# An attention stage in front of two expert layers: masking from PSUM, full-height V products, fp32r flips, and a new order of all steps

## The chip, the cores and the metric

The kernel runs on one core of a Trainium2 chip. The metric is the device time of one execution in microseconds, the median over runs. The engines are TensorE (PE; its weight loads are listed apart as PEld), VectorE (DVE), ScalarE (ACT), GpSimd (POOL) and SyncE (SP), which issues all DMAs here. Each engine works through its own queue in the order in which the program wrote it.

## The reference

Attention over 4 batches x 8 heads, 576 positions, head size 64, with a threshold instead of a full softmax, and then two pairs of dense layers on the 2304 tokens. Cut to what matters:

```python
scores = (1 / sqrt(64)) * q @ k.T                      # 576 x 576 for each head
thresh = max(scores, axis=-1) - tau
scores = where(scores >= thresh, scores, -1e9)
attn   = exp(scores - max(scores)); attn /= sum(attn) + 1e-9
x      = heads side by side of (attn @ v)              # 2304 x 512
h = x @ w_in;  x = (h * sigmoid(1.702 * h)) @ w_out    # 512 -> 2048 -> 512
h = x @ w2_in; y = max(0.01 * h, h) @ w2_out           # 512 -> 2048 -> 512
```

All is fp32, and the weights come as fp64. Precision is kept by splitting an operand into a high half in fp32r (a 32-bit format that TensorE takes in one product) and a low half, the difference.

## The kernel before, in words

Attention goes by head pairs, 16 of them; a pair has two heads of 576 rows, which make nine row tiles of 128 (t = 0 to 8; tile 4 holds the last 64 rows of both heads). For each pair the program has about 130 named steps, each a few instructions on one engine:

- `Lk`, `Lq`, `Lv` load, `dkh`, `dkl`, `dqh`, ... (`divide`, L372 and L377, POOL) split into halves. `fk0` to `fq2` (`flip`, L384, PE) transpose the split q and k, 18 tiles of 128 x 128, `ek`, `eq` (ACT) copy them out of PSUM, `sw` swaps halves of k by DMA.
- For each tile t: `Q` (`scores`, L430, PE) writes minus the scores into one of two PSUM buffers named `s`; `R` (`row_min`, L458, DVE) finds the minimum of the row and writes a copy of the scores to SBUF (`sc`, three buffers); `E` (`exponent`, L471, ACT) takes the exponential from PSUM, behind which the PSUM buffer is free; `T` (`threshold`, L478, in five groups of one or two tiles, four on POOL and one on DVE) adds tau; `S` (`mask`, L492, DVE) multiplies the exponential by "copy of the score <= threshold" and sums the row.
- `P` (`flip_probs`, L513, PE) transposes the masked tile into one of four PSUM banks named `t`; `w` (L535, ACT) copies it to SBUF, `h` (L544, ACT; L540, POOL, for tile 2) makes the high half, `l` (L551, POOL; L549, DVE, for tiles 4 and 6) the low half. `F`, `x`, `y` do the same with the last 64 columns.
- `V` (`values`, L586 and L593, PE) multiplies by v: for each of two row groups (256 and 320 columns), two heads and two halves, four products over 128 rows and one over the 64 rows that are left. `a`, `b` add the halves; `ia`, `ib`, `rb`, `N`, `c` (L662) multiply by the inverse of the row sums and write x.

The order is written out by hand: the table `START` gives each step a number, for the first and last pairs in tables of their own and for the others in one table that is shifted by `PERIOD` from pair to pair; the steps are sorted by these numbers, and thus each engine's queue is made. The steps of two or three neighbouring pairs are interleaved. Into the tables of pair 0 are also written the first six weight blocks of the first layer: `G` loads one, `A` to `K` build fp32 from fp64 bits (L311 on ACT, L313, L315, L319 and L323 on DVE), `H` and `M` split it (ACT, POOL).

The two layers follow from 396 us on: 512-column products on PE, the activation on ACT and DVE, halves on ACT and POOL. Nothing there is changed.

Of the kernel before, what the change touches and what calls it, by code (L numbers as in the profile page):

```python
# [8 lines left out]
F32 = mybir.dt.float32  # L9
F32R = mybir.dt.float32r  # L10
# [24 lines left out]
LO = ("P", "P", "PP", "P", "D", "P", "D", "P", "P")  # L35


THR_ENGINE = "PDPPP"
VB, PPB, SCB = 1, 3, 3
WARM = 8  # L40
PERIOD = 17190
# [21 lines left out]
    },  # L63
    0: {
        "G00": 584, "LkB": 1059, "LkA": 2359, "LqB": 2834, "LqA": 4134, "khB": 4232, "A00": 4592, "Lt": 4609,
# [24 lines left out]
    },  # L90
# [18 lines left out]
    },  # L109
# [130 lines left out]
def attention_moe_moe(  # L240
# [20 lines left out]

    ident = cp.tile([P, P], F32, name="ident")
    make_identity(nc, ident)
    xx_all = cp.tile([P, NCB, NTOK], F32, name="x")
    x = [xx_all[:, c, :] for c in range(NCB)]


# [721 lines left out]
```

## Time and profile before

| | |
|---|---|
| median of 3 runs | 1204.96 us (1204.79 to 1207.99) |
| the profiled execution | 1204.73 us, span 1203.0 us |
| PE, PEld busy over the span | 97%, 81% |
| DVE, ACT, POOL busy over the span | 57%, 49%, 57% |
| last `c` step of attention | 396.4 us after the span's start |

The shares are averages over two unlike stages: in the first third DVE and POOL are over 90% busy, behind it they are at some 40%, and PE is at 98% to 99%.

### The profile page before, as it was taken

The numbers are of one execution on the slowest core, as the hardware profiler recorded it, in microseconds if no ns is written. First come the engines' busy times: TensorE is split into PE (matmuls) and PEld (weight loads), VectorE is DVE, ScalarE is ACT, GpSimd is POOL, SyncE is SP. The second block draws the span as 40 slices with busy tenths as digits, with TensorE's granted clock in tenths as the row PEclk, the third lists the DMA queues.
The fourth block names the chain that finished last, engine by engine and source line by source line (L and its number), as shares of the span: only waits on it lengthen the run. The fifth ranks groups of instructions, "written<-read, shape, count | busy, mean of one in ns | idle before, by whom it ended". The sixth has DMA issues, their size and how long they took to land.

```text
span 1203.0 us, 17030 instructions
## 1 busy us (share of the span) xinstructions
PE 1165.1 (97%) x6169; PEld 970.7 (81%) x6169; DVE 685.8 (57%) x1376; ACT 588.0 (49%) x1090; POOL 688.5 (57%) x606
## 2 busy tenths in 40 slices
PE   6889999999999899999999999999999999999998
PEld 6677888888877688888888888888888888888886
DVE  7999999999999433433534434442343443444222
ACT  6778888888876444333323323344443333333221
POOL 6899999999987655433333433365543433343221
PEclk8999999999998999999999999999999999999999
DMA  4422322312210111101101111110120111110022
GB/s 133 122 66 60 84 56 69 81 50 76 64 40 18 53 36 53 53 18 53 53 25 47 53 36 37 52 53 25 47 57 31 36 53 36 53 36 1 35 62 62
DMA packets 47620, 62.38 MB, mean 52 GB/s; under 512 B 10544, under 2 KB 39216, under 8 KB 47536
## 3 DMA queue, kind: packets, MB, share of 16 engines
q1 hardware_dynamic: 47536, 61.29, 17.9%
q8 instruction: 49, 0.80, 0.3%
q14 instruction: 35, 0.29, 0.1%
HBM read 47.71 MB, written 4.72 MB: 44 GB/s over the span
## 4 chain that ended last, share of the span: by engine, by line
PE 69%; POOL 18%; DVE 6%; issue 4%; ACT 1%; DMA 1%; SPq 0%; DVEq 0%; POOLq 0%; ACTq 0%
PE h L829 31%; PE y L876 16%; PE y L874 15%; POOL ptg0l L551 4%; POOL ptg1l L551 4%; POOL thr L478 2%; PE pv L586 2%; DVE pp L492 2%; POOL rb L635 1%; POOL khl L377 1%; PE s L430 1%; POOL qhl L372 1%; POOL vhl L377 1%; PE pp L513 1%; PE pv L593 1%
## 5 line engine op out<-in xcount | busy, mean ns | idle before, releaser
L845 POOL TENSOR_TENSOR gl<-gf,gh 128x512 fp32r<-128x512 f32 (+1 forms) x160 | 210.1, 1313 | 471.6 <-ACT gh L844 454.9
L841 DVE TENSOR_TENSOR gf<-h,gf 128x512 f32<-128x512 f32 (+1 forms) x80 | 51.0, 637 | 242.0 <-ACT gf L840 242.0
L838 DVE TENSOR_TENSOR gf<-h,gf 128x512 f32<-128x512 f32 (+1 forms) x80 | 51.0, 637 | 231.7 <-ACT gf L837 231.7
L829 PE MATMUL h<-xl,wih 128*128 128x512 f32 (+1 forms) x640 | 159.9, 369 | 3.0 <-POOL xl L818 3.0
L829 PE MATMUL h<-xh,wih 128*128 128x512 f32 (+1 forms) x640 | 158.8, 369 | 1.7 <-ACT xh L817 1.6
L840 ACT ACTIVATE gf<-h 128x512 f32<-128x512 f32 (+1 forms) x80 | 44.4, 555 | 233.7 <-PE h L829 230.6
L829 PE MATMUL h<-xh,wil 128*128 128x512 f32 (+1 forms) x640 | 157.5, 368 | 0.0
L837 ACT ACTIVATE gf<-h 128x512 f32<-128x512 f32 (+1 forms) x80 | 44.3, 554 | 228.1 <-PE h L829 225.0
L492 DVE SCALAR_TENSOR_TENSOR pp<-sc,thr,e 128x576 f32<-128x576 f32 x128 | 151.3, 1191 | 2.3 <-POOL thr L478 1.8
L829 PEld LDWEIGHTS h<-xl,wih 128*128 128x128 f32 x640 | 113.9, 188 | 26.1 <-POOL xl L818 6.1
L829 PEld LDWEIGHTS h<-xh,wih 128*128 128x128 f32 x640 | 114.6, 188 | 24.5 <-ACT xh L817 3.4
L829 PEld LDWEIGHTS h<-xh,wil 128*128 128x128 f32 x640 | 113.8, 189 | 20.0
L471 ACT ACTIVATE e<-s,m 128x576 f32<-128x576 f32 x144 | 107.1, 744 | 34.4 <-DVE sc L458 18.9
L844 ACT CAST gh<-gf 128x512 fp32r<-128x512 f32 (+1 forms) x160 | 92.7, 579 | 56.6 <-DVE gf L841 32.3
L874 PE MATMUL y<-gh,woh 128*128 128x512 f32 (+1 forms) x320 | 117.0, 370 | 2.1 <-DVE x L894 1.2
L874 PE MATMUL y<-gh,wol 128*128 128x512 f32 (+1 forms) x320 | 116.4, 368 | 0.0
L876 PE MATMUL y<-woh,gh 128*128 128x512 f32 x288 | 112.4, 390 | 0.0
L876 PE MATMUL y<-wol,gh 128*128 128x512 f32 x288 | 112.3, 390 | 0.0
L458 DVE TENSOR_SCALAR_CACHE_REDUCE sc<-s 128x576 f32<-128x576 f32 x144 | 107.1, 750 | 3.9 <-PE s L447 1.6
L430 PE MATMUL s<-kt,qt 128*128 128x288 f32 x512 | 99.2, 319 | 9.6 <-ACT e L471 7.4
L551 POOL TENSOR_TENSOR ptg0l<-raw,ptg0h 128x512 fp32r<-128x512 f32 x64 | 91.5, 1431 | 0.3 <-ACT ptg0h L544 0.3
L874 PE MATMUL y<-gl,woh 128*128 128x512 f32 (+1 forms) x320 | 88.5, 368 | 0.0
(122 smaller groups left out, 2261.9 us busy)
## 6 DMA issues: line engine op xcount, KB each, us to landing
w<-in_moe_w_in_dram SPq DMA_DIRECT2D x32, 512.0 KB, 3.7
w<-in_moe_w_out_dram SPq DMA_DIRECT2D x32, 512.0 KB, 3.5
kt<-kt SPq DMA_DIRECT2D x30, 288.0 KB, 4.1
kn<-in_k_dram SPq DMA_DIRECT2D x16, 256.0 KB, 2.8
qn<-in_q_dram SPq DMA_DIRECT2D x16, 256.0 KB, 2.8
vn<-in_v_dram SPq DMA_DIRECT2D x16, 256.0 KB, 3.0
out_dram<-o SPq DMA_DIRECT2D x20, 128.0 KB, 2.4
out_dram<-o SPq DMA_DIRECT2D x8, 256.0 KB, 2.2
```

The source lines that it names most:

```text
L430: nc.tensor.matmul(sc[:, a, 0:HALF], lhsT=w, rhs=kt[n][:, c : c + HALF], start=n == 0, stop=n == 1)
L458: nc.vector.tensor_scalar(out=split(r["sc", t], 2), in0=r["s", t][:, :, 0:HALF], scalar1=1.0, scalar2=3.0e38, op0=ALU.mult, op1=ALU.min, a ...
L471: nc.scalar.activation(split(e, 2), r.pop(("s", t))[:, :, 0:HALF], AF.Exp, bias=r["m"][:, t : t + 1], scale=-1.0)
L492: nc.vector.scalar_tensor_tensor(out=dst, in0=r.pop(("sc", t)), scalar=r["thr"][:, t : t + 1], in1=r.pop(("e", t)), op0=ALU.is_le, op1=ALU ...
L551: nc.gpsimd.tensor_tensor(out=lo, in0=split(st[p].pop(("raw", t)), 4), in1=hi, op=ALU.subtract)
L829: nc.tensor.matmul(h, lhsT=wt[:, c * P : (c + 1) * P], rhs=xx[c], start=i == 0 and c == 0, stop=i == 2 and c == NCB - 1)
L838: nc.vector.tensor_tensor(out=gf, in0=h, in1=gf, op=ALU.mult)
L841: nc.vector.tensor_tensor(out=gf, in0=h, in1=gf, op=ALU.max)
L844: nc.scalar.copy(gh, gf)
L845: nc.gpsimd.tensor_tensor(out=gl, in0=gf, in1=gh, op=ALU.subtract)
L874: nc.tensor.matmul(ys[e][:, 0:w], lhsT=wt[:, at_e], rhs=g, start=first, stop=last)
L876: nc.tensor.matmul(ys[e], lhsT=g[:, at_e], rhs=wt, start=first, stop=last)
```

## The change

- `R` is a reduction that reads the scores in PSUM and writes only the minimum; there is no copy `sc`. `S` reads the scores in PSUM, so a buffer `s` is free only behind `S`.
- `T` is one step for each tile, all nine on DVE.
- Tile 2's high half is made by ACT from PSUM, as for the other tiles.
- v's buffer is one lasting tile that is zeroed once; the last 64 rows of the second head lie in a tenth tile, so that the fifth product of each `V` step runs over all 128 rows, of which 64 are zero. v's split covers ten tiles.
- `flip` is a matmul in fp32r with an fp32r identity in place of a transpose of fp32 bits. `corner` uses two matmuls over all 128 rows in place of a transpose and a matmul over 64.
- All tables of `START` are new, and so is `PERIOD` (17190 to 21444); the numbers serve as sort keys only. Pair 12 uses the common table now, pair 3 too. The weight blocks begin behind the first thresholds of pair 0 (`G00`) and their steps lie among those of pairs 1 to 9; before, four of the six were converted among the first steps and two at the end of attention.

```diff
-LO = ("P", "P", "PP", "P", "D", "P", "D", "P", "P")
-THR_ENGINE = "PDPPP"
-VB, PPB, SCB = 1, 3, 3
-PERIOD = 17190
+LO = ("P", "P", "P", "P", "D", "P", "D", "P", "P")
+PPB = 3
+PERIOD = 21444
...
+    identr = cp.tile([P, P], F32R, name="identr")
+    nc.vector.tensor_copy(identr, ident)
...
+        vn = at.tile([P, 640], F32, name="vn")
+        nc.gpsimd.memset(vn, 0.0)
...
+            c = 320 if nm == "v" else 0
...
-                    nc.sync.dma_start(t[64 * j : 64 * j + 64, 256:320], src[b, h0 + j, 512:576, :])
+                    nc.sync.dma_start(t[64 * j : 64 * j + 64, 256 + c * j : 320 + c * j], src[b, h0 + j, 512:576, :])
...
-            src = st[p][nm + "n"][:, 0:576].rearrange("p (t d) -> p t d", d=D)
+            n = 10 if nm == "v" else 9
+            src = st[p][nm + "n"][:, 0 : n * D].rearrange("p (t d) -> p t d", d=D)
...
-                nc.tensor.transpose(pt[:, n * P : (n + 1) * P], st[p][nm][:, t, :].bitcast(F32), ident)
+                nc.tensor.matmul(pt[:, n * P : (n + 1) * P], lhsT=st[p][nm][:, t, :], rhs=identr, start=True, stop=True)
...
-            r["sc", t] = at.tile([P, S], F32, tag="sc", name=f"sc{p}_{t}", bufs=SCB)
-            nc.vector.tensor_scalar(
-                out=split(r["sc", t], 2),
-                in0=r["s", t][:, :, 0:HALF],
-                scalar1=1.0,
-                scalar2=3.0e38,
-                op0=ALU.mult,
-                op1=ALU.min,
-                accum_out=small(p, "m")[:, t : t + 1],
+            nc.vector.tensor_reduce(
+                out=small(p, "m")[:, t : t + 1], in_=r["s", t][:, :, 0:HALF], axis=mybir.AxisListType.XY, op=ALU.min
             )
...
-        def threshold(p, n):
-            c = slice(THR[n][0], THR[n][-1] + 1)
-            (nc.vector if THR_ENGINE[n] == "D" else nc.gpsimd).tensor_scalar(
+        def threshold(p, t):
+            c = slice(t, t + 1)
+            nc.vector.tensor_scalar(
...
             nc.vector.scalar_tensor_tensor(
-                out=dst,
-                in0=r.pop(("sc", t)),
+                out=split(dst, 2),
+                in0=r.pop(("s", t))[:, :, 0:HALF],
                 scalar=r["thr"][:, t : t + 1],
-                in1=r.pop(("e", t)),
+                in1=split(r.pop(("e", t)), 2),
...
-            nc.tensor.transpose(pt[0:64, 256:320], src[0:64, :], ident[0:64, 0:64])
-            nc.tensor.matmul(pt[64:128, 256:320], lhsT=src[64:128, :], rhs=ident[64:128, 64:128], start=True, stop=True)
+            for h in range(2):
+                d = slice(64 * h, 64 * h + 64)
+                nc.tensor.matmul(pt[d, 256:320], lhsT=src, rhs=ident[:, d], start=True, stop=True)
...
-            for j in range(4):
+            for j in range(5):
                 nc.tensor.matmul(
                     pv,
                     lhsT=r["v"][:, 5 * h + j, :],
-                    rhs=r["pt", gi][n][:, j, h, :],
-                    start=n == 0 and j == 0,
-                    stop=False,
+                    rhs=r["pt", gi][n][:, j, h, :] if j < 4 else r["rt", gi][n],
+                    start=first and j == 0,
+                    stop=not first and j == 4,
                 )
-            nc.tensor.matmul(
-                pv, lhsT=r["v"][rows, 4, :], rhs=r["rt", gi][n][rows, :], start=False, stop=n == 1
-            )
```

The order of the common table in the part that the prediction walks through, by queue (a prime marks the pair before, `+` the pair behind):

```
PE:  Q0 P5' N0' fk0+ P6' Q8' fk2+ Q1 fk1+ P0 P7' fq0+ Q2 F1' P8' Q3 P1 V100' V101' Q4 P2 Q5 ...
DVE: R0 S7' T0 c0' S0 R8' T8' R1 S8' l6' T1 S1 R2 ia1' y1' T2 R3 S2 ib1' T3 S3 b10' R4 ...
ACT: E7' w5' E0 h5' h6' ek0+ ek2+ E8' ek1+ h0 E1 w0 w7' h7' x1' eq0+ E2 h8' E3 ...
```

## Rows read from the trace of the kernel before

**Rows 1.** Windows: length, busy us (count) by engine, clock, DMA share, GB/s.
```profile
10.00:60.00 50.00, 39.23 (x237) 32.77 (x236) 48.81 (x98) 36.17 (x68) 39.99 (x34) 0.90 0.41 116
...
200.00:250.00 50.00, 49.69 (x339) 41.80 (x338) 48.74 (x115) 43.57 (x82) 50.00 (x47) 1.00 0.24 60
...
360.00:396.90 36.90, 33.95 (x185) 25.47 (x183) 30.87 (x71) 24.32 (x47) 26.04 (x26) 0.91 0.09 30
...
600.00:1203.00 603.00, 595.20 (x2805) 498.43 (x2804) 226.55 (x388) 192.85 (x350) 231.89 (x182) 1.00 0.14 42
```
**Rows 2.** The chain that ended last: start us, us, what.
```profile
117.72 1.64 POOL rb L635 x3
...
228.37 1.64 POOL rb L635 x3
```
**Rows 3.** Waits, four pairs, 150.2 to 238.7 us: total, times, longest.
```profile
PEld s L430 <- ACT e L471: 1.4, 4, 0.3
PEld pp L513 <- DVE xs L612: 0.8, 4, 0.2
```
**Rows 4.** VectorE by line and form, same stretch: busy us, mean ns | idle before.
```profile
L492 DVE SCALAR_TENSOR_TENSOR pp<-sc,thr,e 128x576 f32<-128x576 f32 x33 | 38.2, 1166 | 0.1
L458 DVE TENSOR_SCALAR_CACHE_REDUCE sc<-s 128x576 f32<-128x576 f32 x36 | 26.8, 751 | 1.2 <-PE s L447 0.7
...
L492 DVE SCALAR_TENSOR_TENSOR pm<-sc,thr,e 128x576 f32<-128x576 f32 x4 | 5.6, 1405 | 0.0
L549 DVE TENSOR_TENSOR ptg1l<-pp,ptg1h 128x512 fp32r<-128x512 f32 x8 | 5.5, 685 | 0.1
...
L478 DVE TENSOR_SCALAR thr<-m,tau_p 128x2 f32<-128x2 f32 x4 | 0.9, 214 | 0.0
```
**Rows 5.** The mask's line, whole run: duration ns min/median/max, first and last start.
```profile
L492 DVE SCALAR_TENSOR_TENSOR pp<-sc,thr,e x128: 798/1197/1892, 14.1 to 381.6; 128x576 f32<-128x576 f32 x128
```
**Rows 6.** POOL and ScalarE by line and form, 150.2 to 238.7 us.
```profile
L471 ACT ACTIVATE e<-s,m 128x576 f32<-128x576 f32 x36 | 26.7, 743 | 4.7 <-DVE sc L458 3.5 <-DVE pp L492 0.9
...
L478 POOL TENSOR_SCALAR thr<-m,tau_p 128x2 f32<-128x2 f32 x12 | 7.5, 623 | 0.0
L544 ACT CAST ptg0h<-pp 128x512 fp32r<-128x512 f32 x12 | 7.1, 595 | 1.4 <-PE pp L513 1.4
...
L540 POOL TENSOR_SCALAR ptg0h<-raw 128x512 fp32r<-128x512 f32 x4 | 4.5, 1122 | 0.0
L478 POOL TENSOR_SCALAR thr<-m,tau_p 128x1 f32<-128x1 f32 x4 | 1.2, 296 | 0.0
```
**Rows 7.** TensorE's timeline: start us, us to the modelled end, instructions.
```profile
204.36 0.77 PE L430 MATMUL s<-kt,qt 128*128 128x288 f32 x4
204.97 0.63 PE L586 MATMUL pv<-ptg0h,vhl 128*128 128x256 f32 x4
205.53 0.38 PE L593 MATMUL pv<-rtg0h,vhl 64*128 64x256 f32 x1
205.84 0.74 PE L586 MATMUL pv<-ptg0l,vhl 128*128 128x256 f32 x4
206.51 0.38 PE L593 MATMUL pv<-rtg0l,vhl 64*128 64x256 f32 x1
206.82 0.44 PE L563 MATMUL pr<-ident,pp 128*128 128x128 f32 x2
```
**Rows 8.** Timeline of weight loads: start us, us, instructions.
```profile
208.95 0.19 PEld L445 LDWEIGHTS s<-kt,qm 128*128 128x128 f32 x1
...
209.57 0.19 PEld L447 LDWEIGHTS s<-kt,qm 128*128 128x128 f32 x1
...
209.87 0.91 PEld L384 LDWEIGHTS pt_q<-ident,qhl 128*128 128x128 f32 x8
210.75 0.57 PEld L430 LDWEIGHTS s<-kt,qt 128*128 128x128 f32 x4
```
**Rows 9.** Weight conversion on VectorE, 0 to 60 us, longest and shortest of four.
```profile
L313 DVE TENSOR_SCALAR wF<-wF 128x512 f32<-128x512 f32 x4 | 4.1, 1034 | 0.1
...
L315 DVE TENSOR_SCALAR wF<-wF 128x512 int32<-128x512 int32 x4 | 2.5, 616 | 0.0
```

More of the change, by code (lines that the diff above doesn't have):

```diff
@@ L32 @@
 HI_MAX = 15 * 2.0**13 - 2.0**-7
-LO = ("P", "P", "PP", "P", "D", "P", "D", "P", "P")
-THR_ENGINE = "PDPPP"
-VB, PPB, SCB = 1, 3, 3
+LO = ("P", "P", "P", "P", "D", "P", "D", "P", "P")
+PPB = 3
 WARM = 8
-PERIOD = 17190
+PERIOD = 21444
 START = {
     "each": {
[17 rows of a table removed]
-    },
-    0: {
-        "G00": 584, "LkB": 1059, "LkA": 2359, "LqB": 2834, "LqA": 4134, "khB": 4232, "A00": 4592, "Lt": 4609,
[24 rows of a table removed]
-    },
[18 rows of a table removed]
-    },
[18 rows of a table removed]
-    },
[18 rows of a table removed]
-    },
[20 rows of a table removed]
+        "Lk": -32936, "dkh": -31433, "dkl": -29771, "Lq": -22850, "dqh": -18694, "dql": -15685, "fk0": -15539,
[16 rows of a table added]
+    },
+    0: {
+        "LkA": -164893, "LkB": -164793, "khA": -164693, "klA": -164593, "khB": -164493, "LqA": -164393,
+        "whA": -164293, "LqB": -164193, "klB": -164093, "Lt": -163993, "wlA": -163893, "fk2": -163793, "whB": -163693,
[25 rows of a table added]
+    },
[18 rows of a table added]
+    },
[18 rows of a table added]
     },
     13: {
[19 rows of a table removed]
+        "Lk": 228107, "Lq": 245817, "dkh": 246850, "dkl": 250182, "dqh": 259894, "dql": 260974, "fk2": 261852,
[18 rows of a table added]
     },
     14: {
[19 rows of a table removed]
[19 rows of a table added]
     },
     15: {
[19 rows of a table removed]
[19 rows of a table added]
     },
@@ L359, in load_part @@
                 for j in range(2):
-                    nc.sync.dma_start(t[64 * j : 64 * j + 64, 256:320], src[b, h0 + j, 512:576, :])
+                    nc.sync.dma_start(t[64 * j : 64 * j + 64, 256 + c * j : 320 + c * j], src[b, h0 + j, 512:576, :])
         def load(p, nm):
-            t = at.tile([P, 640], F32, tag=nm + "n", name=f"{nm}n{p}")
+            t = vn if nm == "v" else at.tile([P, 640], F32, tag=nm + "n", name=f"{nm}n{p}")
             for part in "AB":
@@ L368, in divide @@
         def divide(p, nm, half):
-            src = st[p][nm + "n"][:, 0:576].rearrange("p (t d) -> p t d", d=D)
+            n = 10 if nm == "v" else 9
+            src = st[p][nm + "n"][:, 0 : n * D].rearrange("p (t d) -> p t d", d=D)
             if half == "h":
-                st[p][nm] = at.tile([P, 9, P], F32R, tag=nm + "hl", name=f"{nm}hl{p}", bufs=VB if nm == "v" else 1)
+                st[p][nm] = at.tile([P, n, P], F32R, tag=nm + "hl", name=f"{nm}hl{p}", bufs=1)
                 nc.gpsimd.tensor_scalar(
@@ L415, in attention_moe_moe @@
         SLOT = [(0, 0), (0, 1), (1, 0), (1, 1), None, (2, 0), (2, 1), (3, 0), (3, 1)]
-        THR = ((0, 1), (2, 3), (4,), (5, 6), (7, 8))
         def scores(p, t):
@@ L471, in exponent @@
             nc.scalar.activation(
-                split(e, 2), r.pop(("s", t))[:, :, 0:HALF], AF.Exp, bias=r["m"][:, t : t + 1], scale=-1.0
+                split(e, 2), r["s", t][:, :, 0:HALF], AF.Exp, bias=r["m"][:, t : t + 1], scale=-1.0
             )
             r["e", t] = e
-        def threshold(p, n):
-            c = slice(THR[n][0], THR[n][-1] + 1)
-            (nc.vector if THR_ENGINE[n] == "D" else nc.gpsimd).tensor_scalar(
+        def threshold(p, t):
+            c = slice(t, t + 1)
+            nc.vector.tensor_scalar(
                 out=small(p, "thr")[:, c], in0=st[p]["m"][:, c], scalar1=tau_p[:, 0:1], scalar2=None, op0=ALU.add
@@ L580, in values @@
             w = GW[gi]
-            if n == 0:
+            first = ("pv", gi, h) not in r
+            if first:
                 r["pv", gi, h] = bank(f"pv{p}_{gi}{h}")
             pv = r["pv", gi, h][:, 0:w]
-            rows = slice(64 * h, 64 * h + 64)
-            for j in range(4):
+            for j in range(5):
                 nc.tensor.matmul(
@@ L683, in attention_moe_moe @@
             step(f"E{t}", exponent, t)
+            step(f"T{t}", threshold, t)
             step(f"S{t}", mask, t)
@@ L689, in attention_moe_moe @@
             step(f"l{t}", probs_lo, t)
-        for n in range(5):
-            step(f"T{n}", threshold, n)
         for gi in range(2):
@@ L790, in attention_moe_moe @@
                 todo += [(t, name, p) for name, t in table.items()]
-        for _, name, p in sorted(todo, key=lambda z: z[0]):
+        for _, name, p in sorted(todo, key=lambda z: (z[0], z[2], z[1])):
             fn, args = (FIRST if p == 0 else STEPS)[name]
```

301 rows, old and new, of the table START are left out of this document.

## The prediction

> **What bounds the kernel now.** I read the busy time by stretches first, then the chain that ended last, then the waits of four steady head pairs. The reader is to see three stages: a start, a steady attention stage, and the two expert layers behind 396 us, whose code the diff leaves alone. In the steady stage POOL is busy 50.00 of 50 us, VectorE 48.74, and TensorE's busy time is 49.69 at granted clock 1.00; ScalarE has room with 43.57 [rows 1]. The chain there is almost wholly POOL's, and the same three-instruction piece of it returns from 117.72 to 228.37 us in five steps: 110.65 / 5 = 22.13 us per head pair [rows 2]. POOL never waits in that stretch. TensorE's weight loads wait for others only 1.4 and 0.8 us in four pairs (a third wait of 0.6 stands below them), 2.8 / 4 = 0.7 us per pair [rows 3]. So three engines are full within 3%: relieving one alone would buy nothing, and the question is how far all of them come down together, and what the new order leaves idle.
>
> **VectorE, per pair of 22.13 us** (busy 48.74 / 50 of it, 21.6).
> The mask: 36 of them took 38.2 + 5.6 = 43.8 us, 1.22 us each [rows 4], and the spread is what matters: 798 ns at the shortest, 1197 at the median, 1892 at the longest [rows 5]. A step of fixed size that takes up to 2.4 times its shortest is being held up, and the instruction that reads one operand from PSUM, the 128x512 subtraction, shows no such thing (685 ns on average beside a full POOL) [rows 4]. With the scores read in PSUM the mask becomes of that kind: 685 x 576/512 = 770 ns. Saved 9 x (1.22 - 0.77) = 4.0 us. Bounds: nothing (if the hold-up comes from the other operand, still in SBUF, or the output) and 9 x 0.47 = 4.2.
> The row minimum: the form that also writes a copy takes 751 ns from PSUM [rows 4]; a reduction passes over the same 576 columns, so I take the same, 0. Bounds: -1 and +1 us for nine of them.
> The threshold: nine one-column steps on VectorE in place of one of two columns at 214 ns [rows 4]: 8 x 0.21 = +1.7. Bounds: +0.9 and +3 (it stands right behind the reduction whose result it reads).
> Sum 21.6 - 4.0 + 1.7 = 19.3.
>
> [...]
>
> **POOL.** Gone are the thresholds, 7.5 + 1.2 = 8.7 us in four pairs, 2.2 per pair, and the high half of tile 2, 1122 ns [rows 6]. v's two divides run over ten tiles instead of nine, some 0.2 more. 22.1 - 2.2 - 1.1 + 0.2 = 19.0. If masks and POOL steps held each other up, POOL's own steps shorten too; I leave that at nothing and keep 1 us for the low end.
>
> **ScalarE** takes over that high half: one cast of 595 ns [rows 6], 43.57 / 50 x 22.13 = 19.3 plus 0.6 = 19.9. Its records overlap a little, so it is not full at that. It stays beside the others; it is the cover that is thinnest.
>
> **TensorE.** Each last product of a V group uses 64 rows. In the timeline four products of 256 columns and one such go 204.97, 205.53, 205.84, 206.51, 206.82: 1.85 us for ten [rows 7], where the 64-row one holds the engine 0.31 us. As full-height products ten would flow at the rate inside a group, 0.56 / 4 = 0.14 at most, 1.4 us, or at the 0.107 that 256 columns take when half of an expert layer's 512-column product is taken (595.20 us for 2805 of them, 0.212 [rows 1]). Saved 0.45 to 0.8 per group, four groups: 1.8 to 3.2 us; I take 2.2.
> The flips: 18 per pair. As fp32 transposes eight weight loads went out between 209.87 and 210.75, 0.11 each; as fp32r products each needs a load of the fp32r kind, and six short products in a row spaced these from 208.95 to 209.57, 0.62 / 5 = 0.12 [rows 8]. 18 x 0.012 = +0.2 us; bounds -0.9 (a product of half the passes, 0.05 less each) and +0.9. The corner keeps about its cost: three small instructions become full-height ones, 0 within 0.3.
> 22.1 - 0.7 - 2.2 + 0.2 = 19.4.
>
> **What the new order leaves idle.** All four engines come to 19 to 20 us, so none will be full. New is that a score buffer (there are two) is held from the product until the mask, where it was free after the exponential. One tile then holds its buffer for the product 0.61 (204.36 to 204.97 [rows 7]) and some 0.15 behind it, the minimum 0.75, the exponential 0.74 [rows 6], the mask 0.77 and some 0.3 of hand-overs: 3.3 us. Nine tiles on two buffers need 15 us, so it fits if VectorE and ScalarE come to them in time. I walked the new order by hand with these durations. The longest gap: tile 7's flip reuses the bank of tile 6, which VectorE frees late with that tile's low half; behind this flip TensorE has a q flip and the scores of tile 2, about 0.42 + 0.45 + 0.61 + 0.15 = 1.6 us, while VectorE has a threshold and a mask, 1.0, so it idles 0.6. Another 0.3 is lost where four copies on ScalarE stand ahead of tile 8's exponential, and several spots are tight. VectorE's 19.3 plus 0.9 is 20.2; ScalarE at 19.9 will add waits of its own, and I take 20.7. Gain 22.13 - 20.7 = 1.43 us over some 14 pairs between ramps: 20 us.
>
> **Weight conversion and ramps.** Before, four of the six early weight blocks are converted within the first 60 us: four VectorE steps each, 616 to 1034 ns, about 3.3 us a block, 13 us [rows 9], in a stretch where VectorE is busy 48.81 of 50 us and TensorE only 39.23 [rows 1]. Now they come behind head pair 0 and spread over pairs 1 to 9, with their loads: SP issues each block between two head loads, and the DMA share in the steady stage is 0.24 [rows 1]. The start gains up to 13; the six blocks, 20 us at most, fall on the idle time just worked out (9 x 1.4 = 13), so some 10 come back. Net gain 3, bounds -5 and +12. The tail (360 to 396.9, clock 0.91 [rows 1]) keeps its chain of flips, low parts, V products and the inverse: 0, within 3.
>
> **Sum.** The profiled execution took 1204.73 us (span 1203.0), 0.2 below the median of the runs, 1204.96. 1204.7 - 20 - 3 = 1182.
>
> **Rivals.**
> 1. The engines do get to their sums. The period is then ScalarE's or TensorE's 19.5 to 20, and 16 pairs gain 2.3 each: 37 us, about 1165. For it: low parts on POOL would also shorten. Against: two buffers and one more hand-over per tile. Chance 0.15.
> 2. Slower, by the score buffers. If other VectorE work queued between a tile's minimum and its mask stretches the hold from 3.3 to over 22.13 x 2 / 9 = 4.9 us on average, the buffers set a period longer than before. Each 0.1 us above that costs 0.45 us per pair. At 5.3 the period is 23.9 and the time 1205 + 14 x 1.8 = 1230. For it: the new order often puts another tile's minimum, an addition and a threshold (some 1.5 us) between the two. Against: that makes 4.8 only if it happened to every tile, and then not more. Chance 0.09.
> 3. The mask does not speed up, its other operand being in SBUF still. VectorE then has 21.6 + 1.7 = 23.3, less what goes into its idle time: 23.3 - 22.1 = 1.2 x 14 = +17, less the 3 of the start, 1219. If it speeds up by half, VectorE with its gaps comes to 22.1 and the time is about 1202. The steady 685 ns row speaks against both. Chance 0.10, 0.04 for no gain at all and 0.06 for half of it.
>
> **How the numbers follow.** My forecast has 0.66: 1182, its own range 1168 to 1198 (the bounds of VectorE's and TensorE's terms move the period by 0.7 either way, the start by 8). A change under 0.3% (3.6 us) can't be told from none here. Faster by more: 0.64 of the forecast, all 0.15 of the first rival and 0.03 of the third, 0.82. Within: 0.02 and 0.03, 0.05. Slower: 0.09 and 0.04, 0.13. Range 1162 to 1205; what lies outside is the slower rivals and the far end of the first.
>
> **What would show it.** The mask at 750 to 800 ns with little spread; no threshold on POOL, and POOL under 90% busy in the steady stage; no 64-row product; the period near 20.7, with VectorE's idle time put down to the exponential and to the scores. It is wrong in its main step if the mask stays above 1 us, and wrong in its order if the masks are short and the period is still 22.

## The result, and the profile after

The changed kernel takes 1178.69 us in the median (1178.28 to 1179.12, four runs), beside 1206.47 us (1204.79 to 1208.78) of the kernel before: a ratio of 0.977 [0.975, 0.979]. The forecast was 1182, range 1162 to 1205. The time is close; the way to it is not the one that was forecast. The profiled execution took 1179.12 us, span 1177.3.

In front of the last step of attention lies the whole difference. Start and length (us) of the last `c` step (L662 before, L619 after) of pairs 0, 1, 2, 8, 12 and 15, from VectorE's timeline of the kernel before:

```profile
65.26 0.48 DVE L662 TENSOR_TENSOR x<-pn,xs 128x320 f32<-128x320 f32 x1
...
101.80 0.48 DVE L662 TENSOR_TENSOR x<-pn,xs 128x320 f32<-128x320 f32 x1
...
124.25 0.48 DVE L662 TENSOR_TENSOR x<-pn,xs 128x320 f32<-128x320 f32 x1
...
256.99 0.48 DVE L662 TENSOR_TENSOR x<-pn,xs 128x320 f32<-128x320 f32 x1
...
345.99 0.48 DVE L662 TENSOR_TENSOR x<-pn,xs 128x320 f32<-128x320 f32 x1
...
396.40 0.49 DVE L662 TENSOR_TENSOR x<-pn,xs 128x320 f32<-128x320 f32 x1
```

and the same steps of the kernel after, with pairs 9 and 10 besides (254.78, 276.47):

```profile
45.75 0.48 DVE L619 TENSOR_TENSOR x<-pn,xs 128x320 f32<-128x320 f32 x1
...
64.68 0.48 DVE L619 TENSOR_TENSOR x<-pn,xs 128x320 f32<-128x320 f32 x1
...
93.21 0.48 DVE L619 TENSOR_TENSOR x<-pn,xs 128x320 f32<-128x320 f32 x1
...
233.10 0.48 DVE L619 TENSOR_TENSOR x<-pn,xs 128x320 f32<-128x320 f32 x1
...
254.78 0.48 DVE L619 TENSOR_TENSOR x<-pn,xs 128x320 f32<-128x320 f32 x1
...
276.47 0.48 DVE L619 TENSOR_TENSOR x<-pn,xs 128x320 f32<-128x320 f32 x1
...
318.77 0.48 DVE L619 TENSOR_TENSOR x<-pn,xs 128x320 f32<-128x320 f32 x1
...
370.58 0.49 DVE L619 TENSOR_TENSOR x<-pn,xs 128x320 f32<-128x320 f32 x1
```

By the differences of these starts the first three pairs gain 124.25 - 93.21 = 31.0 us; pairs 3 to 8 give 139.9 - 132.7 = 7.1 back; pairs 9 to 12 gain 89.0 - 85.7 = 3.3; the last three lose 51.8 - 50.4 = 1.4. Together 25.8, and the spans differ by 25.7.

These ends do not mark the same amount of work in both orders, because the new order brings a pair's last step sooner behind its masks: at the end of pair 2, 40 masks had begun before and 34 after. There are 144 masks in all, so one can count by them instead. VectorE's busy time on the mask's line (L492 before, L451 after) in front of the 28th mask, counted with the short record behind each of the 27 (length, busy, count, clock, DMA share, GB/s), before and after:

```profile
0.00:92.00 92.00, 33.88 (x54) 0.94 0.37 105
```

```profile
0.00:74.70 74.70, 21.76 (x54) 1.00 0.42 112
```

Starts in us from VectorE's timelines; the last three columns are experiments that follow below:

| start of | before | after | after_early | copy_mask | no_conv |
|---|---|---|---|---|---|
| 1st mask | 14.11 | 12.57 | 22.48 | 12.74 | 12.43 |
| 28th mask | 92.08 | 74.72 | 92.14 | 84.32 | 74.01 |
| 118th mask | 314.11 | 305.73 | 308.40 | 331.47 | 290.32 |
| 144th mask | 381.59 | 363.82 | 367.42 | 395.40 | 348.39 |
| last `c` step | 396.40 | 370.58 | 380.17 | 402.59 | 355.17 |

By this count the start gains 17.4 us, the 90 masks behind it lose 231.0 - 222.0 = 9.0, the last 26 masks gain 9.4, and what follows the last mask gains 8.0.

A steady pair without weight steps takes 276.47 - 254.78 = 21.69 us, where 22.13 [rows 2] became a forecast 20.7.

Windows of the kernel after (columns as in [rows 1]): the start, one steady pair, the layers.

```profile
10.00:60.00 50.00, 44.13 (x337) 40.66 (x336) 46.40 (x116) 44.86 (x88) 38.55 (x36) 1.00 0.45 113
...
259.80:281.50 21.70, 20.13 (x152) 18.11 (x152) 20.91 (x51) 19.20 (x38) 16.24 (x16) 1.00 0.26 71
...
600.00:1177.00 577.00, 569.50 (x2681) 476.63 (x2679) 220.50 (x376) 185.67 (x338) 224.17 (x175) 1.00 0.14 43
```

POOL went from full to 16.24 of 21.70 us, 75%. VectorE alone is nearly full, with 20.91. The layers run as before.

Lines by form of the kernel after, three pairs, 238.13 to 303.1 us (columns as in [rows 4]):

```profile
L423 DVE TENSOR_REDUCE m<-s 128x1 f32<-128x576 f32 x27 | 20.3, 753 | 0.3 <-PE s L396 0.2
L451 DVE SCALAR_TENSOR_TENSOR pp<-s,thr,e 128x576 f32<-128x576 f32 x25 | 20.3, 812 | 1.2 <-ACT raw L494 0.5
...
L437 DVE TENSOR_SCALAR thr<-m,tau_p 128x1 f32<-128x1 f32 x28 | 5.6, 200 | 0.1
...
L580 DVE TENSOR_SCALAR inv<-sum 128x5 f32<-128x5 f32 x3 | 3.5, 1167 | 0.0
...
L580 DVE TENSOR_SCALAR inv<-sum 128x4 f32<-128x4 f32 x3 | 2.7, 897 | 0.0
```

Mask, minimum and threshold have the forecast sizes. The surprise stands in the last two rows: `ia`, the addition of 1e-9 to four or five columns of row sums, which the diff leaves alone but for its place in the order. The same form in four pairs of the kernel before, 150.2 to 238.7 us:

```profile
L623 DVE TENSOR_SCALAR inv<-sum 128x5 f32<-128x5 f32 x4 | 0.6, 158 | 0.0
L623 DVE TENSOR_SCALAR inv<-sum 128x4 f32<-128x4 f32 x4 | 0.6, 155 | 0.0
```

It grew from 0.158 + 0.155 = 0.31 to 1.167 + 0.897 = 2.06 us per pair. The kernel before had a sign of it outside its steady pairs, in the longest of the same line over the whole run:

```profile
L623 DVE TENSOR_SCALAR inv<-sum x32: 154/158/1386, 27.8 to 383.9; 128x4 f32<-128x4 f32 x16, 128x5 f32<-128x5 f32 x16
```

VectorE's and POOL's timelines of the kernel after show by what:

```profile
266.11 0.93 DVE L580 TENSOR_SCALAR inv<-sum 128x5 f32<-128x5 f32 x1
...
271.20 1.27 DVE L580 TENSOR_SCALAR inv<-sum 128x4 f32<-128x4 f32 x1
```

```profile
265.73 1.28 POOL L510 TENSOR_TENSOR ptg1l<-raw,ptg1h 128x512 fp32r<-128x512 f32 x1
...
271.15 1.29 POOL L510 TENSOR_TENSOR ptg0l<-raw,ptg0h 128x512 fp32r<-128x512 f32 x1 [0.15 <-DMA kn<-in_k_dram]
```

Both additions start inside a low part of POOL and end within 0.03 us of its end: 267.04 with 267.01, 272.47 with 272.44. The mask no longer behaves so (line L451, whole run, columns as in [rows 5]), nor does the one-column threshold of the same kind of instruction:

```profile
L451 DVE SCALAR_TENSOR_TENSOR pp<-s,thr,e x128: 780/810/824, 12.6 to 363.8; 128x576 f32<-128x576 f32 x128
```

```profile
L437 DVE TENSOR_SCALAR thr<-m,tau_p x144: 164/205/217, 12.2 to 363.1; 128x1 f32<-128x1 f32 x144
```

So the mask, 798 to 1892 ns long with its scores in SBUF [rows 5], takes 780 to 824 with them in PSUM, and the addition, which reads and writes SBUF alone, took 150 to 1293 ns (line L580, whole run). Why the one-column step goes free, no run here shows.

### The profile page after: what moved, and what is told of

Read it like the earlier page. It is cut to its first block, busy times and chain, and to the rows that moved or that the text cites. A ratio compares the mean times of both kernels' runs of the same rounds, so it can differ in the third digit from the quotient of the medians.

```text
span 1177.3 us, 16994 instructions
## 1 busy us (share of the span) xinstructions
PE 1126.4 (96%) x6201; PEld 963.3 (82%) x6201; DVE 660.0 (56%) x1361; ACT 587.9 (50%) x1106; POOL 598.4 (51%) x527
## 3 DMA queue, kind: packets, MB, share of 16 engines
q1 hardware_dynamic: 47536, 61.29, 18.4%
## 4 chain that ended last, share of the span: by engine, by line
PE 70%; DVE 16%; ACT 7%; issue 4%; POOL 2%; DMA 1%; SPq 0%; DVEq 0%; ACTq 0%; POOLq 0%
PE h L785 32%; PE y L832 17%; PE y L830 15%; DVE pp L451 4%; DVE m L423 3%; PE pv L546 2%; ACT e L430 2%; DVE inv L580 2%; PE s L396 1%; ACT ptg1h L503 1%; DVE xs L569 1%; ACT raw L494 1%; DVE ptg1l L508 1%; ACT kt L366 1%; PE pp L472 1%
## 5 line engine op out<-in xcount | busy, mean ns | idle before, releaser
L800 ACT CAST gh<-gf 128x512 fp32r<-128x512 f32 (+1 forms) x160 | 92.7, 579 | 57.4 <-DVE gf L797 32.4
L430 ACT ACTIVATE e<-s,m 128x576 f32<-128x576 f32 x144 | 107.8, 752 | 25.8 <-DVE m L423 23.4
L423 DVE TENSOR_REDUCE m<-s 128x1 f32<-128x576 f32 x144 | 107.7, 751 | 4.4 <-PE s L396 2.1
L451 DVE SCALAR_TENSOR_TENSOR pp<-s,thr,e 128x576 f32<-128x576 f32 x128 | 103.5, 810 | 3.8 <-ACT e L430 0.8
L396 PEld LDWEIGHTS s<-kt,qt 128*128 128x128 f32 x512 | 72.9, 190 | 30.7 <-DVE pp L451 18.1
L510 POOL TENSOR_TENSOR ptg0l<-raw,ptg0h 128x512 fp32r<-128x512 f32 x64 | 83.2, 1309 | 22.1 <-ACT raw L494 20.4
```

Of the source, the lines that this page charges most:

```text
L396: nc.tensor.matmul(sc[:, a, 0:HALF], lhsT=w, rhs=kt[n][:, c : c + HALF], start=n == 0, stop=n == 1)
L423: nc.vector.tensor_reduce(out=small(p, "m")[:, t : t + 1], in_=r["s", t][:, :, 0:HALF], axis=mybir.AxisListType.XY, op=ALU.min)
L430: nc.scalar.activation(split(e, 2), r["s", t][:, :, 0:HALF], AF.Exp, bias=r["m"][:, t : t + 1], scale=-1.0)
L451: nc.vector.scalar_tensor_tensor(out=split(dst, 2), in0=r.pop(("s", t))[:, :, 0:HALF], scalar=r["thr"][:, t : t + 1], in1=split(r.pop(("e" ...
L510: nc.gpsimd.tensor_tensor(out=lo, in0=split(st[p].pop(("raw", t)), 4), in1=hi, op=ALU.subtract)
L800: nc.scalar.copy(gh, gf)
```

## The experiments

All ratios are to the kernel before, measured anew beside each run.

**The addition alone, on ScalarE (ia_act).** It takes from VectorE the one step that grew; if the order and its waits set the period, the time stays.

```diff
-                nc.vector.tensor_scalar(
-                    out=iv, in0=st[p]["sum"][:, c], scalar1=1e-9, scalar2=None, op0=ALU.add
-                )
+                nc.scalar.activation(iv, st[p]["sum"][:, c], AF.Copy, bias=1e-9)
```

> The changed kernel with the addition of 1e-9 to the row sums on ScalarE instead of VectorE. In the changed kernel this step of 4 or 5 columns takes 0.9 and 1.2 us on VectorE in the steady pairs, and ends when a POOL instruction ends. If VectorE bounds the steady pairs (96 to 98% busy) and that is a hold-up, about 1.8 us per pair come free and 1.0 to 1.8 of them are gained: 1152 to 1166, pairs at 20 to 20.7 us instead of 21.7. If TensorE, ScalarE or the two score buffers bind next, it is 1170 to 1180.

Measured 1162.59 us (1161.77 to 1163.6), 0.964 [0.961, 0.966]: 16.1 less than the changed kernel. Timeline of two ends of pairs, window over these two pairs, and the addition's line:

```profile
220.38 0.48 DVE L617 TENSOR_TENSOR x<-pn,xs 128x320 f32<-128x320 f32 x1
...
261.20 0.48 DVE L617 TENSOR_TENSOR x<-pn,xs 128x320 f32<-128x320 f32 x1
```

```profile
220.40:261.20 40.80, 39.70 (x306) 36.47 (x306) 38.35 (x98) 38.54 (x80) 33.68 (x34) 1.00 0.31 81
```

```profile
L580 ACT ACTIVATE inv<-sum x32: 205/223/280, 18.5 to 350.0; 128x4 f32<-128x4 f32 x16, 128x5 f32<-128x5 f32 x16
```

The period is 40.82 / 2 = 20.41 us, 1.28 less. The addition was on the path with most of its 1.75 us. Now TensorE is the fullest, 39.70 of 40.80.

**The mask reads a copy again (copy_mask)**, in the new order. Two things come back with the copy: the score buffer is free behind the exponential, and a record of 80 ns follows each minimum (0.7 us per pair). All else is as changed.

```diff
-            nc.vector.tensor_reduce(out=small(p, "m")[:, t : t + 1], in_=r["s", t][:, :, 0:HALF],
-                axis=mybir.AxisListType.XY, op=ALU.min)
+            r["sc", t] = at.tile([P, S], F32, tag="sc", name=f"sc{p}_{t}", bufs=2)
+            nc.vector.tensor_scalar(out=split(r["sc", t], 2), in0=r["s", t][:, :, 0:HALF], scalar1=1.0,
+                scalar2=3.0e38, op0=ALU.mult, op1=ALU.min, accum_out=small(p, "m")[:, t : t + 1])
...
-                in0=r.pop(("s", t))[:, :, 0:HALF],
+                in0=split(r.pop(("sc", t)), 2),
```

> The changed kernel and its order, but the row minimum writes a copy of the scores to SBUF again (two buffers) and the mask reads that copy; the score buffer is free behind the exponential again. If the mask was what VectorE gained (about 0.4 us for each of nine masks, 3.7 us per pair, VectorE over 95% busy in the changed kernel), it takes 1178.7 + 16 x 2.5 to 3.7, so 1218 to 1238, with the mask at 1.1 to 1.3 us and a longest near 1.9. If the gain came from the other parts and the order alone, it stays below 1190.

Measured 1209.32 us (1208.37 to 1211.11), 1.002 [1.001, 1.004], 30.6 above the changed kernel: without the masks from PSUM, and what comes with them, nothing is left of the gain. The time lies somewhat below the expected range. The mask's line, whole run and then 278.3 to 345 us (three pairs), with the addition:

```profile
L458 DVE SCALAR_TENSOR_TENSOR pp<-sc,thr,e x128: 798/840/2121, 12.7 to 395.4; 128x576 f32<-128x576 f32 x128
```

```profile
L458 DVE SCALAR_TENSOR_TENSOR pp<-sc,thr,e 128x576 f32<-128x576 f32 x24 | 24.6, 1024 | 0.7
...
L587 DVE TENSOR_SCALAR inv<-sum 128x5 f32<-128x5 f32 x3 | 2.3, 773 | 0.0
...
L587 DVE TENSOR_SCALAR inv<-sum 128x4 f32<-128x4 f32 x3 | 1.2, 385 | 0.0
```

Of the 32.0 us by which its attention ends later (402.59 less 370.58), the first three pairs hold 12.5 (105.68 less 93.21), pairs 3 to 8 8.3, pairs 9 to 12 5.5 and the last three 5.8, but its pairs 11 and 12 take 22.1 and 21.8 us against 21.1 and 21.2. So this part is worth 4.2 us per pair in the start, or 9.6 us by the count of masks (84.32 - 74.72), and (8.3 + 5.5) / 10 = 1.4 per pair in the ten pairs behind it. In settled pairs half of the hold-up is gone in the new order with the copy too (1.02 us, not 1.22), and the additions are shorter there: what is held changes place.

**The weight blocks.** Three kernels: the changed one with the weight steps back among the first and the last steps of attention ("after_early"), the old one with them at the new places ("before_late"), and the changed one without the VectorE steps of the six early blocks ("no_conv"). In the first two only keys of the weight steps change, of which three are shown:

```diff
 after_early, START[0]:
-"G00": -44637   "B00": 36838    "M21": 220839
+"G00": -80366   "B00": -75593   "M21": 384403
 before_late, START[0]:
-"G00": 584      "B00": 5357     "M21": 292502
+"G00": 10996    "B00": 37409    "M21": 183331
```

> The changed kernel with the steps of the six early weight blocks put back where they stood in the order before (four blocks among the steps of pairs 0 and 1, the rest at the end of attention). Theory A, the move out of the start is what made the ramp shorter: pair 0 ends 10 to 15 us later than in the changed kernel (45.75 us), pairs 2 to 8 come at 21.7 us instead of 23.3 to 25, and the time is 1182 to 1195. Rival B, the ramp is shorter because of the other parts (masks that nothing holds up, another order): pair 0 ends near 50 us, the pairs behind it gain, and the time is 1165 to 1175.

Measured 1189.0 us (1188.86 to 1189.15), 0.986 [0.983, 0.988], 10.3 more than the changed kernel. Ends of pairs 2, 8, 12 and 15: 106.93, 235.75, 321.42, 380.17. Against the changed kernel's 93.21, 233.10, 318.77, 370.58 the start is 13.7 longer, pairs 3 to 8 are 11.1 shorter, pairs 9 to 12 equal, and the last three 6.9 longer, where two blocks now lie again.

Not all of the 13.7 and the 10.3 is the move's, because this edit does not bring the old start back. The kernel before issues its first weight load ahead of all others, this one behind those of the first pair (start us, us, before first); VectorE then waits for the block in front of its first minimum (its longest wait in 0 to 23 us):

```profile
0.72 0.44 SPq L297 DMA_DIRECT2D w<-in_moe_w_in_dram  x1
```

```profile
12.66 0.59 SPq L251 DMA_DIRECT2D w<-in_moe_w_in_dram  x1
```

```profile
DVE wF L267 <- ACT wF L265: 6.1, 1, 6.1
```

Its first mask begins at 22.48 us, against 14.11 before and 12.57 after. What the move alone is worth in the new order is therefore not shown; 10.3 less the 6.1 us of this wait leaves about 4, an estimate.

> The kernel before with one thing changed: the steps of the six early weight blocks stand where the changed kernel has them, spread over pairs 1 to 9. Theory A, the later place is a gain only because the other parts made room in the steady pairs: the start gets shorter (last c step of pair 0 at 45 to 50 us, from 65.3), but POOL and VectorE are full in the steady pairs, which lengthen by 3 to 4 us for each block, and the time is 1198 to 1212. Rival B, the later place is a gain by itself: 1188 to 1197, as much as the 10 us that it is worth in the changed kernel.

Measured 1221.39 us (1217.48 to 1228.57), 1.013 [1.008, 1.017]: in the old order the move costs about 15, more than either theory's range. Some 13 of it stand at a like clock: with a mean granted clock of 0.992 and 0.993 this kernel took 1218.37 and 1217.48 us, the kernel before beside it, with 0.992, 1204.82 and 1205.04. In the profiled execution (1224.41 us, clock 0.984) pairs 3 to 8 take 273.86 - 119.13 = 154.7 us, 22 more than before; the granted clock was 0.93 in them, where it had been 1.00, so up to 0.07 x 155 = 11 us of the 22 may be the clock's, an estimate. VectorE's masks are held for 1205 ns there still, and the steps find no room (lines by form, then the longest wait, 174.4 to 250 us):

```profile
L484 DVE SCALAR_TENSOR_TENSOR pp<-sc,thr,e 128x576 f32<-128x576 f32 x24 | 28.8, 1205 | 1.6 <-POOL thr L470 1.6
```

```profile
POOL thr L470 <- DVE sc L450: 7.4, 5, 2.0
```

So the parts do not add up one by one: what pays or costs little behind the others is a loss without them.

```diff
-  FIRST[f"{part}{f}{n}"] = (lambda p, *z: convert(*z), (1, f, n, part))
+  FIRST[f"{part}{f}{n}"] = (lambda p, *z: z[3] in "BCDK" or convert(*z), (1, f, n, part))
```

> The changed kernel without the four VectorE steps of the conversion of each of the six early weight blocks (those layers' first weights are then wrong; all else is done). Pairs 2 to 8 took 23.3 to 25.1 us where the later ones took 21.7. If the VectorE steps are the cause, these pairs come at 21.7 and the time is 1178.7 - 8 to 14, so 1165 to 1171. If it is the loads, ScalarE's two steps or POOL's one that are in their way, it stays above 1174.

Measured 1164.3 us (1162.83 to 1166.85), 0.966 [0.963, 0.969]: the 24 steps cost 14.4 us, somewhat more than expected. Left out, pairs 3 to 8 take 217.69 - 89.11 = 128.6 us, 11.3 less, and pairs 9 to 12 still 21.7, 21.7, 21.1, 21.2. The conversion is the reason for the long middle, not for the period.

The two together (ia_no_conv: addition on ScalarE, conversion steps left out):

> The changed kernel with the addition of 1e-9 on ScalarE and without the four VectorE steps of the conversion of the six early weight blocks (the first weights of the layers are then wrong). In the changed kernel leaving them out was worth 14.4 us. If VectorE is what they fill, and it has 1.3 us more room per pair now, they cost less: 8 to 12 us, 1150 to 1155, with pairs 2 to 8 at 20.4 us. If they cost the same 14, VectorE is full in either kernel: 1147 to 1149.

Measured 1152.43 us (1151.81 to 1153.44), 0.955 [0.951, 0.958], 10.2 under the addition alone. The two effects overlap by 14.4 - 10.2 = 4.2: with room on VectorE the same steps cost less.

**v's short tiles (v64).** Nine tiles again, each group's last product over 64 rows, in the new order.

```diff
-            n = 10 if nm == "v" else 9
+            n = 9
...
-            for j in range(5):
+            rows = slice(64 * h, 64 * h + 64)
+            for j in range(4):
...
+            nc.tensor.matmul(pv, lhsT=r["v"][rows, 4, :], rhs=r["rt", gi][n][rows, :], start=False, stop=not first)
```

> The changed kernel with the V products as before: nine tiles of v, and the fifth product of each V step over the 64 rows of one head. Theory A, TensorE does not bound the changed kernel's steady pairs (it is idle 1.6 us of 21.7 there, waiting for masks): the 1.8 to 2.2 us more per pair are mostly hidden, and the time is 1178 to 1186. Rival, as the prediction took it, TensorE is as near to the bound as VectorE: 1178.7 + 14 x 1 to 2, 1192 to 1207.

Measured 1197.05 us (1194.23 to 1201.84), 0.992 [0.989, 0.995]: 18.4 more than the changed kernel. My theory's range failed and the rival's held. The `V` groups on TensorE, first the changed kernel, then this one, ten products each:

```profile
276.57 0.64 PE L546 MATMUL pv<-ptg0h,vhl 128*128 128x256 f32 x4
277.05 0.28 PE L546 MATMUL pv<-rtg0h,vhl 128*128 128x256 f32 x1
277.17 0.64 PE L546 MATMUL pv<-ptg0l,vhl 128*128 128x256 f32 x4
277.65 0.28 PE L546 MATMUL pv<-rtg0l,vhl 128*128 128x256 f32 x1
277.76 0.64 PE L546 MATMUL pv<-ptg0h,vhl 128*128 128x256 f32 x4
```

```profile
264.28 0.64 PE L547 MATMUL pv<-ptg0h,vhl 128*128 128x256 f32 x4
264.86 0.38 PE L550 MATMUL pv<-rtg0h,vhl 64*128 64x256 f32 x1
265.17 0.73 PE L547 MATMUL pv<-ptg0l,vhl 128*128 128x256 f32 x4
265.83 0.38 PE L550 MATMUL pv<-rtg0l,vhl 64*128 64x256 f32 x1
266.14 0.73 PE L547 MATMUL pv<-ptg0h,vhl 128*128 128x256 f32 x4
```

277.76 - 276.57 = 1.19 us against 1.86; the 64-row product holds TensorE 0.31 us, the full one 0.12. The pair takes 23.2 to 23.3 us, and over two pairs (columns as in [rows 1]) TensorE is the fullest engine, 45.04 of 46.50 us, with VectorE at 42.34:

```profile
240.80:287.30 46.50, 45.04 (x305) 37.23 (x304) 42.34 (x101) 38.77 (x76) 33.07 (x34) 1.00 0.27 71
```

The longer groups reach VectorE by way of ScalarE's copy `sh` (waits, 245 to 311 us):

```profile
ACT sh L559 <- PE pv L550: 7.1, 6, 1.6
DVE xs L567 <- ACT sh L559: 5.2, 4, 1.5
```

**The flips** as transposes of fp32 bits again, in the changed kernel (flip32) and beside the addition on ScalarE (ia_flip32).

```diff
-  nc.tensor.matmul(pt[:, n * P : (n + 1) * P], lhsT=st[p][nm][:, t, :], rhs=identr, start=True, stop=True)
+  nc.tensor.transpose(pt[:, n * P : (n + 1) * P], st[p][nm][:, t, :].bitcast(F32), ident)
```

> The changed kernel with q and k flipped by transposes of fp32 bits again. By the rows of before and after a flip costs TensorE 0.10 to 0.12 us either way; expected 1176 to 1181, no difference that this measurement can tell. If products in place of transposes were worth 0.05 us each, 18 per pair, and TensorE bound, it would be 1190.

Measured 1177.76 us (1177.72 to 1177.94), 0.976 [0.974, 0.978].

> The changed kernel with the addition of 1e-9 on ScalarE (1162.6 so far) and with the flips as fp32 transposes. If TensorE has become nearer to the bound with pairs at 20.4 us, a difference between the two kinds of flip shows: 18 per pair by 0.01 to 0.05 us, 2 to 12 us either way. If not, 1161 to 1164.

Measured 1163.42 us (1162.63 to 1164.72), 0.964 [0.961, 0.967]. Against the same kernels with fp32r flips: -0.9 and +0.8 us. The flips are worth nothing either way.

**An attempt at more (best_b)**: the addition on ScalarE, and one of the four conversion steps of the early blocks (part B, L275) on POOL.

```diff
-  nc.vector.tensor_scalar(out=F, in0=F, scalar1=2.0**-15, scalar2=HI_MAX, op0=ALU.max, op1=ALU.min)
+  (nc.gpsimd if layer == 1 and f < NA else nc.vector).tensor_scalar(
+      out=F, in0=F, scalar1=2.0**-15, scalar2=HI_MAX, op0=ALU.max, op1=ALU.min)
```

> The changed kernel with the addition of 1e-9 on ScalarE, as in the run before (1162.6), and with the clamp of the six early weight blocks (one of the four VectorE steps of the conversion, 0.41 us by itself, up to 1.25 beside POOL) on POOL, which is busy 75% of the steady pairs. If VectorE still bounds the pairs with conversion (21 to 24 us, where the others took 20.4), 3 to 6 us are gained: 1156 to 1160. If POOL's step blocks others for as long, it is 1161 to 1165.

Measured 1164.2 us (1163.01 to 1164.41), 0.964 [0.963, 0.966]: nothing gained over the addition alone, though POOL has room. The best measured version that computes all of the reference is the one with the addition on ScalarE, 1162.59 us, under both kernels.

## Why the prediction was right and wrong

The step that failed is the last of "What the new order leaves idle": "I take 20.7. Gain 22.13 - 20.7 = 1.43 us". A steady pair gained 0.44. Over pairs 3 to 12 the gain was 3.3 - 7.1 = -3.8 us, but there the weight steps are in it, which the prediction priced apart; with these left out ("no_conv") the ten pairs take 303.34 - 89.11 = 214.2 us against 221.7, a gain of 7.5, or 0.75 per pair. That is half of what was forecast.

The terms of that step, per pair, forecast and measured:

| | forecast | measured |
|---|---|---|
| VectorE busy | 19.3 | 20.9 |
| VectorE idle | 1.4 | 0.8 |
| TensorE busy | 19.4 | 20.1 |
| ScalarE busy | 19.9 | 19.2 |
| POOL busy | 19.0 | 16.2 |

It was VectorE's sum that failed. From the rows: masks 9 x (1.217 - 0.811) = -3.65, thresholds 9 x 0.200 - 0.214 = +1.59, minimum 0 (751 and 753 ns), the addition +1.75; together -0.31. The three terms that the prediction priced each came out within 0.4 us. The fourth was missing: a step which the diff only moves was counted at its old 0.16 us, though the argument for the mask was that VectorE instructions are held up beside POOL. (The account is rough: VectorE's busy time fell by 21.6 - 20.9 = 0.7, neighbouring records overlap, and the 80 ns records behind each minimum went too.) With that one step taken off VectorE ("ia_act") it is busy 38.35 / 2 = 19.2 us per pair and the period is 20.4: the forecast 19.3 and 20.7 nearly hold, and that run supports the rest of the step. The first rival's 1165 was reached too, but only by this edit, which the diff lacks.

Why the addition was not held in the steady pairs before, when POOL was full, the old trace shows: the one at 213.17 us began there 0.12 us before a POOL instruction ended, and so, by 0.05 to 0.13 us, did all 18 between 124.65 and 301.88 us (154 to 160 ns each). Where the order of the first pairs put it elsewhere, the same addition was held in the same kernel: from 78.90 to 80.28 us, beside a POOL step that ended at 80.26. The old place was a lucky one and not a safe one, and the row's longest, 1386 ns, said so before the change.

The weight conversion: "The start gains up to 13 ... some 10 come back. Net gain 3". That some 10 come back nearly holds: "no_conv" gives 11.3 in pairs 3 to 8 and 14.7 in the 90 masks. The gain of the start is not shown apart, for the 13.7 of "after_early" hold a wait of 6.1 us that the kernel before did not have. Of the six blocks two stood before at the end of attention, and the 6.9 that they cost there in "after_early" was left out by the term "tail ... 0"; by masks, what follows the last mask took 14.8 us before and 6.8 after.

The start: no gain was put there but the conversion's. It gained 17.4 by masks, of which 9.6 go with the masks from PSUM by "copy_mask"; the 31.0 at the end of pair 2 hold besides that a pair's last step now comes sooner. The prediction spread the masks' gain over the 14 steady pairs alone. That it is larger in the start because POOL has idle time there and VectorE almost none ([rows 1], 10 to 60 us) is argued and not shown.

So 1182 came near 1178.7 by luck in the sum. The forecast was 20 + 3 = 23; by masks the 25.8 are 17.4 in the start, -9.0 in the 90 masks behind it, 9.4 in the last 26 and 8.0 behind the last mask. The -9.0 are 14.7 lost to the weight steps (231.0 less the 216.3 of "no_conv") and 5.7 gained. Of the 9.4, 5.8 go with the masks from PSUM (63.9 in "copy_mask" against 58.1), and of the 8.0, 6.0 with the two blocks (12.8 in "after_early" against 6.8); the rest stays open.

Right by the runs: that the mask is held up with its scores in SBUF (up to 1892 ns before, 2121 in "copy_mask") and not with them in PSUM (up to 824), its size (0.77 forecast, 0.81), the third rival refuted, the flips at nothing, the full-height products (2.2 forecast, 4 x 0.66 = 2.6 on TensorE). They are worth 18.4 us, and without them TensorE is the fullest engine (97% busy in "v64"). POOL at 16.2 is below the 19.0 worked out: the shortening of its own steps that I left "at nothing" came. Its low parts of the first kind (`ptg0l`) went from 1422 to 1309 ns, and the high half of k from 975 to 687 (means over the first 360 us of each kernel). The slower rival of the score buffers did not come true: TensorE's waits for a mask to free a buffer come to 2.5 + 4.7 us in three pairs on its two queues, which may lie side by side, and "ia_act" reaches 20.4 with the same two buffers.

## What to carry to other kernels

Where two engines hold each other up, cost every instruction of the full engine, the unchanged small ones too, at its held duration as soon as the order moves: a step that lasted 0.16 us in one order took 1.2 in another. Read the longest of a row over the whole run, not only the mean of the steady stage: it can show the hold-up that a lucky place hides. Look for the gain stage by stage, by a count of work that means the same in both orders. And test the parts in the order in which they are to run: the move of the weight steps cost 13 to 15 us in the old order, where the new one lost up to 10 without it.

## What the runs showed of the hardware

- A VectorE `tensor_scalar` over four or five fp32 columns in SBUF was held to the end of a running POOL instruction, up to 1293 ns after the change and 1386 before. After it 24 of the 32 took 0.24 to 1.29 us and ended 0.02 to 0.04 us behind the end of a POOL step, and the other eight took 0.15 to 0.17. The one-column form (one at 267.35 us, inside a POOL step from 266.97 to 268.40) never took over 217 ns, and the reciprocal of the same four or five columns took 0.16 to 0.18 us. What sets these apart wasn't found.
- The conversion's own steps are held too: L281, with two SBUF operands, takes 679 ns at the shortest and 1989 at the longest, this one from 180.68 us beside a POOL step from 180.56 to 182.12, with its end 0.55 us behind that step's. With POOL idle, at 47.01 us, it took 0.68.
- The granted clock was 0.93 on average in two stretches of the changed kernel, 168 to 191 and 194 to 218 us, where TensorE was busy 20.27 of 23 and 21.04 of 24 us. In 186 to 188 and 210 to 212 us it was 0.50; shortly before, TensorE had been busy only 0.76 of 2 us (182 to 184) and 0.68 of 2 us (206 to 208). What lowers it is not shown.
- That clock costs little here: with the fp32 flips ("flip32") it was 1.00 over the same pairs (92.7 to 231.6 us; over the whole run 0.999, against 0.995), weight steps and all, and pairs 3 to 8 took 138.9 us where the changed kernel's took 139.9. So of the 11.3 us that "no_conv" gains in them about 1 is the clock's and the rest the steps', an estimate.
